# The decay mask of a retention block: made on the chip from two loaded rows instead of loaded as a table

## The chip, the cores and the metric

One core of one Trainium2 chip. The metric is device time in microseconds (us) of one execution; lower is better. Several executions are given by their median. Times inside an execution come from one profiled execution, counted from the start of its span.

## The reference

Three stages follow one another on 2 x 768 tokens: a retention (linear attention with a fixed decay for each of 8 heads of 64 channels), an MLP 512 -> 2048 -> 512 with x·sigmoid(1.702x), and a SwiGLU 512 -> 1536 -> 512 behind an RMS norm.

```python
gamma = 1.0 - 2.0 ** (-5.0 - np.arange(H))
for t in range(S):
    state = gamma * state + outer(k[:, :, t], v[:, :, t])
    y[:, :, t] = scale * (q[:, :, t] @ state)
h = y @ w_in;  x1 = (h * sigmoid(1.702 * h)) @ w_out
xn = x1 / sqrt(mean(x1 ** 2) + 1e-6) * rms_g
out = (silu(xn @ w_gate) * (xn @ w_val)) @ w_out2
```

The MLP's and the SwiGLU's weight matrices arrive as 64-bit floats; the kernel brings them to float32 on the chip.

## The kernel before

The retention is computed in 12 chunks of 128 tokens (6 for each of the two sequences). Within a chunk, the scores of k and q for the 8 heads are one product (L319, 8 calls in float32, which the trace shows as 16 matmuls; even heads lie on partitions 0 to 63 and odd ones on 64 to 127), and VectorE multiplies them by a constant table, the decay mask `dm_sb` of 128 x 2 x 4 x 128 float32 (L333): scale·gamma^(t-s) where the query's token t is not before the key's token s, and 0 elsewhere. The masked scores times v give the output of the chunk (`intra`, L369); for all chunks but a sequence's first there is a second part from the state (`inter`, L356), which reads `qd`, the queries times `qd_sb` (made by GpSimd, L281). The state is brought on by `update_products` (L413), which reads `kd`, the keys times `sm_sb` (GpSimd, L288), by a decay on ScalarE (L421) and a sum on VectorE (L429, L431).

The opening (L850 to L965) is written out by hand: the loads, then chunks 0 to 3 of the retention mixed with the conversion of the first weights (tiles `w`, L189 to L222), and the first product of the MLP (`in_proj`, L467). `in_order(opening)` (L965) keeps the instructions of TensorE, VectorE, ScalarE and GpSimd in the order in which the opening writes them; SP's DMA queue isn't in that list. Everything behind the opening is put in order by a scheduler when the program is built; instructions of later lines may be placed among the opening's where their engine is free and nothing orders them. Two of these are on ScalarE: `mean_w` (L1075) and the scaling of the RMS norm's weights in place, `g_sb` (L1076).

Nearly all loads are issued by SP's queue, in the order of the code: q and k of chunk 0 (`qk`, 512 KB), one half of the mask (256 KB), qk of chunk 1, the other half, v and k of chunk 0 (`kv`, two pieces), v of chunk 1, `qd_sb`, qk of chunk 2, and so on to the tiles of chunk 5. ScalarE's queue issues two small ones: `sm_sb` (12 numbers on each of 128 partitions, 6 KB) and `g_sb` (4 numbers on each, 2 KB). The first work of TensorE are 8 products of a constant (`warming(WARM)`, L859), whose result nobody reads.

Of the kernel before, what the change touches and what calls it, by code (L numbers as in the profile page):

```python
# [8 lines left out]
F32 = mybir.dt.float32  # L9
# [6 lines left out]
ALU = mybir.AluOpType  # L16
# [3 lines left out]
C = 128  # L20
NC = S // C
NP = H // 2
DM = H * D
NT = B * S
KD = DM // 128
F1 = 2048 // 128
F2 = 1536 // 128
T = 512
# [14 lines left out]
WITH_WR = (0, 1, 2, 3, 4, 5, 6, 10, 11, 12)  # L43
JOIN = 4
HELD = 2
WARM, MORE = 8, 0
ENGINES = [mybir.EngineType.PE, mybir.EngineType.DVE, mybir.EngineType.Activation, mybir.EngineType.Pool]
SPLIT = [mybir.EngineType.DVE, mybir.EngineType.Activation]
WAIT = mybir.DependencyInfo(mybir.DependencyClass.Sync, mybir.DependencyReason.DATA)
# [4 lines left out]
def tile_retention_mlp_swiglu(  # L54
# [19 lines left out]
    nc = tc.nc  # L74
# [6 lines left out]
    xt_p = pool("xt", 1)  # L81
# [5 lines left out]
    ps_t = pool("ps_t", 2, space=PSUM)  # L87
# [6 lines left out]
    dm_sb = at_p.tile([128, 2, NP, C], F32, name="dm_sb")  # L94
    qd_sb = at_p.tile([128, NP, C], F32, name="qd_sb")
    S_two = [at_p.tile([128, NP, D], F32, name=f"S_sb{n}") for n in range(2)]
    sm_sb = const.tile([128, 12, 1], F32, name="sm_sb")
    g_sb = const.tile([128, KD], F32, name="g_sb")
# [9 lines left out]
    def psum(p, name):  # L108
        return p.tile([128, T], F32, tag=p.name, name=name)
# [156 lines left out]
    def load_kv(c, parts=None):  # L266
        if ("kv", c) not in ld:
            p, tag = (wr_p, "wr") if c < CPB else (ld_p, "ld")
            ld["kv", c] = p.tile([128, 2, H, D], F32, tag=tag, name=f"kv{c}")
        t = ld["kv", c]  # L270
        if parts is None and c >= 2:
            nc.sync.dma_start(out=t.rearrange("p a h d -> p (a h d)"), in_=kv[c])
            return
        for n in parts or (1, 0):
            nc.sync.dma_start(out=t[:, n].rearrange("p h d -> p (h d)"), in_=kv[c][:, n * T:n * T + T])
# [36 lines left out]
    def score_products(c, p):  # L312
        t = ld["qk", c]
        sc = at["sc", c] = [psum(p, f"sc{c}_{e}") for e in range(2)]
        begun = len(nc.cur_bb.bb.instructions)
        earlier = of(mybir.EngineType.PE)[-1]
        for n in range(NP):
            for e in range(2):
                nc.tensor.matmul(  # L319
                    out=sc[e][:, n * C:(n + 1) * C],  # L320
                    lhsT=t[64 * e:64 * e + 64, 1, n, :],
                    rhs=t[64 * e:64 * e + 64, 0, n, :],
                    start=True,
                    stop=True,
                )
        if c > CPB:
            after(of(mybir.EngineType.PE, begun)[0], earlier)

    def masks(c):
        sc = at.pop(("sc", c))  # L330
        for e in range(2):
            a = tmp(f"a{c}_{e}")
            nc.vector.tensor_tensor(  # L333
                out=a, in0=sc[e], in1=dm_sb[:, e].rearrange("p n c -> p (n c)"), op=ALU.mult
            )
            at["a", c, e] = a
# [373 lines left out]
    fill = deque()  # L710
# [146 lines left out]
    def warming(n):  # L857
        for _ in range(n):
            nc.tensor.matmul(out=warm, lhsT=one(128), rhs=one(T), start=True, stop=True)  # L859

    def load_mask(e):
        o = slice(e * T, e * T + T)
        nc.sync.dma_start(out=dm_sb.rearrange("p e n c -> p (e n c)")[:, o], in_=dmask[:, o])

    warming(WARM)
    load_qk(0)
    load_mask(0)
    load_qk(1)
    load_mask(1)
    load_kv(0)  # L870
    nc.scalar.dma_start(out=sm_sb.rearrange("p n o -> p (n o)"), in_=small)
    load_kv(1, (1,))
    nc.sync.dma_start(out=qd_sb.rearrange("p n c -> p (n c)"), in_=qdec)
    load_qk(2)
# [4 lines left out]
    load_kv(3)  # L879
    for _ in range(3):  # L880
        load_next()
    nc.scalar.dma_start(out=g_sb, in_=rms_g)
    load_qk(CPB)
    load_kv(CPB)
    load_qk(CPB + 1)
    load_kv(CPB + 1)

    nc.scalar.activation(out=first, in_=ones[:, 0:1], func=ACTF.Silu)
    score_products(0, ps_a)
    score_products(1, ps_a)  # L890
    warming(MORE)
    masks(0)
    prep_k(0)
    intra(0, ps_h)
    masks(1)
# [16 lines left out]
    r = convert_next(split=True)  # L912
# [461 lines left out]
```

## Time and profile before

| | us |
|---|---|
| median of three executions (lowest, highest) | 585.52 (585.43, 586.13) |
| the profiled execution, its own time | 585.22 |
| its span | 583.4 |
| TensorE busy in the span | 575.7 |

The span runs from the first to the last instruction of the profiled execution; its own time holds 1.82 us more. A matmul's busy time includes waiting in TensorE's pipeline, so that two of them overlap; what the engine did not do is read from the idle times.

### The profile page before, as it was taken

To read this page: it belongs to the slowest core of one execution; us is meant where nothing else is said; L and a number is where in the kernel's file an instruction comes from. 1 tells how busy PE (TensorE), PEld (TensorE's weight loads), DVE (VectorE), ACT (ScalarE), POOL (GpSimd) and SP (SyncE) were. 2 spreads that over 40 slices of the span, in tenths; PEclk is the share of its full clock that TensorE was granted. 3 is DMA by queue.
4 is the path that set the end of the run, shared out by engine and by line. 5 is a ranking of instruction groups with operands and counts; after the bars stand their busy time and mean duration, and the time that the engine had idled before them with its cause. 6 is when DMAs were issued, how large, how long until landed. Compare 5 with 4: busy or idle time off the path is not lost.

```text
span 583.4 us, 9280 instructions
## 1 busy us (share of the span) xinstructions
PE 575.7 (99%) x3274; PEld 481.1 (82%) x3274; DVE 450.7 (77%) x806; ACT 365.4 (63%) x697; POOL 24.5 (4%) x26
## 2 busy tenths in 40 slices
PE   7999999999999999999999999999999999999997
PEld 5887887888788888878888888988989889988885
DVE  3899998879989888367998998888958676644542
ACT  2878776667687887466647875666645446634442
POOL 3300212100000000000000000000000000000000
PEclk9999999999999999999999999999999999999999
DMA  8999999888369899878744336676414476560412
GB/s 321 408 287 379 391 325 370 276 258 311 115 238 317 285 328 349 306 246 315 290 162 165 108 122 203 200 230 220 163 61 138 145 273 247 201 207 11 152 65 74
DMA packets 48287, 135.11 MB, mean 232 GB/s; under 512 B 5616, under 2 KB 5872, under 8 KB 48240
## 3 DMA queue, kind: packets, MB, share of 16 engines
q1 hardware_dynamic: 47808, 134.37, 66.0%
q8 instruction: 26, 0.43, 0.3%
q14 instruction: 21, 0.17, 0.1%
q10 hardware_dynamic: 432, 0.14, 0.1%
HBM read 98.84 MB, written 35.65 MB: 231 GB/s over the span
## 4 chain that ended last, share of the span: by engine, by line
PE 97%; DMA 2%; ACT 0%; DVE 0%; issue 0%; ACTq 0%
PE acc L444 8%; PE h L467 8%; PE acc L446 7%; PE acc L445 7%; PE o L444 6%; PE o L445 6%; PE o L446 6%; PE sc L319 2%; PE y L356 2%; PE y L369 2%; DMA qk<-in_qk 1%; PE m7a L778 1%; PE v0a L778 1%; PE m0a L778 1%; PE m1a L778 1%; PE g10a L778 1%
## 5 line engine op out<-in xcount | busy, mean ns | idle before, releaser
L445 PE MATMUL o<-w,gh 128*128 128x512 f32 x144 | 56.2, 390 | 0.0
L444 PE MATMUL o<-w,gh 128*128 128x512 f32 x144 | 56.2, 390 | 0.0
L446 PE MATMUL o<-w,gl 128*128 128x512 f32 x144 | 56.1, 389 | 0.0
L201 DVE CUSTOM_DVE_ANT_0 qw<-qw,uw 128x1024 uint16<-128x1024 uint16 x67 | 45.9, 686 | 2.6 <-ACT uw L199 0.5
L198 ACT ACTIVATE qw<-w 128x512 f32<-128x512 f32 x67 | 44.6, 665 | 2.6 <-DMA w<-in_w 2.6
L199 ACT ACTIVATE uw<-w 128x512 uint32<-128x512 uint32 x67 | 44.7, 668 | 0.0
L450 DVE TENSOR_TENSOR gl<-gw,gh 128x512 fp32r<-128x512 f32 x24 | 16.6, 691 | 27.1 <-ACT gh L449 27.0
L200 DVE TENSOR_SCALAR qw<-qw 128x512 uint32<-128x512 uint32 x67 | 28.8, 431 | 9.9 <-ACT qw L198 9.8
L449 ACT ACTIVATE gh<-gw 128x512 fp32r<-128x512 f32 x24 | 15.1, 630 | 28.0 <-PE o L445 22.5
L446 PEld LDWEIGHTS o<-w,gl 128*128 128x128 f32 x144 | 27.0, 188 | 5.7
L445 PEld LDWEIGHTS o<-w,gh 128*128 128x128 f32 x144 | 27.1, 188 | 4.6
L444 PEld LDWEIGHTS o<-w,gh 128*128 128x128 f32 x144 | 27.1, 188 | 4.5
L444 PE MATMUL acc<-gh,wo 128*128 128x512 f32 x64 | 25.9, 412 | 0.0
L446 PE MATMUL acc<-gh,wo 128*128 128x512 f32 x64 | 25.0, 391 | 0.0
L445 PE MATMUL acc<-gl,wo 128*128 128x512 f32 x64 | 25.0, 391 | 0.0
L445 PE MATMUL acc<-gl,wowp 128*128 128x512 f32 x64 | 24.9, 389 | 0.0
L446 PE MATMUL acc<-gh,wowp 128*128 128x512 f32 x64 | 24.9, 389 | 0.0
L444 PE MATMUL acc<-gh,wowq 128*128 128x512 f32 x64 | 24.9, 389 | 0.0
L445 PE MATMUL acc<-gl,wowq 128*128 128x512 f32 x64 | 24.9, 389 | 0.0
L446 PE MATMUL acc<-gh,wowq 128*128 128x512 f32 x64 | 24.9, 389 | 0.0
L207 DVE SCALAR_TENSOR_TENSOR qw<-w,qw 128x512 uint32<-128x512 uint32 x36 | 24.7, 686 | 0.2
L467 PE MATMUL h<-xt0h,wih 128*128 128x512 f32 (+2 forms) x68 | 24.8, 387 | 0.0
(1519 smaller groups left out, 1691.4 us busy)
## 6 DMA issues: line engine op xcount, KB each, us to landing
w<-in_w SPq DMA_DIRECT2D x68, 512.0 KB, 6.2
qk<-in_qk SPq DMA_DIRECT2D x12, 512.0 KB, 7.6
kv<-in_kv SPq DMA_DIRECT2D x10, 512.0 KB, 8.5
gmd<-gm SPq DMA_DIRECT2D x16, 256.0 KB, 4.4
gwm<-gmd SPq DMA_DIRECT2D x16, 256.0 KB, 4.5
g1d<-gs SPq DMA_DIRECT2D x12, 256.0 KB, 2.1
g2d<-gl SPq DMA_DIRECT2D x12, 256.0 KB, 2.6
gw<-g1d SPq DMA_DIRECT2D x12, 256.0 KB, 3.4
```

What stands on the lines that cost most here:

```text
L198: lambda: nc.scalar.activation(out=q, in_=high.bitcast(F32), func=ACTF.Copy, scale=2.0 ** -112),
L199: lambda: nc.scalar.activation(out=t, in_=low, func=ACTF.Copy, scale=2.0 ** -29),
L200: lambda: nc.vector.tensor_scalar(out=m, in0=m, scalar1=3, scalar2=None, op0=ALU.logical_shift_left),
L201: lambda: nc.vector.tensor_tensor(out=m, in0=m, in1=t, op=ALU.add),
L207: nc.vector.scalar_tensor_tensor(out=dst, in0=high, scalar=0x80000000, in1=m, op0=ALU.bitwise_and, op1=ALU.bitwise_or)
L444: nc.tensor.matmul(out=out, lhsT=ah, rhs=bh, start=first, stop=False)
L445: nc.tensor.matmul(out=out, lhsT=ah, rhs=bl, start=False, stop=False)
L446: nc.tensor.matmul(out=out, lhsT=al, rhs=bh, start=False, stop=last)
L449: nc.scalar.activation(out=hi, in_=src, func=ACTF.Copy)
L450: nc.vector.tensor_tensor(out=lo, in0=src, in1=hi.bitcast(F32), op=ALU.subtract)
L467: nc.tensor.matmul(out=ps[:, begin:end], lhsT=w[a][:, k * 128:(k + 1) * 128], rhs=x[b][:, k, begin:end], start=begin == 0 and o == order[0 ...
L778: nc.tensor.matmul(out=bank, lhsT=u, rhs=v, start=first and k == 0 and x == 0, stop=k == 1 and x == 2, skip_group_check=True,)
```

## The change

Both halves of the mask's load go away. Instead:

- ScalarE's queue loads two things into a tile called `rows`, on partitions 0 and 64 alone: the whole of `small` (1536 numbers, its first eight columns being gamma_h^(127-s) by token s and head h) and one row of `qdec` (512 numbers, scale·gamma_h^(t+1) by head pair and token t) for the even and for the odd heads.
- VectorE fills the mask's tile with gamma_h^(-128) (8 memsets), and GpSimd sets it to 0 where the query's token lies before the key's (2 affine_selects).
- TensorE makes 8 outer products of one partition each (float32, 128 x 128), whose stationary operand is read from `rows` in steps of 12 numbers, into two PSUM tiles; VectorE multiplies each by the constant triangle, in place (2 operations of 128 x 512).
- These products stand ahead of chunk 0's scores on TensorE, and the two multiplications ahead of chunk 0's masking on VectorE.
- `sm_sb` is loaded third on ScalarE's queue, behind that engine's first activation, where it was the first.
- `g_sb` is loaded by SP's queue behind the tiles of chunk 5, where ScalarE's queue loaded it second.
- 6 warming products stand where there were 8; `masks(0)` is written ahead of chunk 1's scores (each engine's own order stays as it was by that).

```diff
-WARM, MORE = 8, 0
+WARM, MORE = 6, 0
...
-    def load_mask(e):
-        o = slice(e * T, e * T + T)
-        nc.sync.dma_start(out=dm_sb.rearrange("p e n c -> p (e n c)")[:, o], in_=dmask[:, o])
+    rows = xt_p.tile([128, KD, T], F32, tag="xt1h", name="rows")
+    by_token = rows[:, 0:3, :].rearrange("p k t -> p (k t)").rearrange("p (t n) -> p t n", n=12)
+    ends_of = slice(0, 65, 64)
+    nc.scalar.dma_start(
+        out=rows[ends_of, 0:3, :].rearrange("p k t -> p (k t)"),
+        in_=small.rearrange("t n -> (t n)").unsqueeze(0).to_broadcast([2, 12 * C]),
+    )
+    nc.scalar.dma_start(out=rows[ends_of, 3, :], in_=qdec[ends_of, :])
+    for e in range(2):
+        for n in range(NP):
+            nc.vector.memset(dm_sb[:, e, n, :], (1.0 - 2.0 ** (-5.0 - (2 * n + e))) ** -C)
+        nc.gpsimd.affine_select(
+            out=dm_sb[:, e], in_=dm_sb[:, e], pattern=[[0, NP], [1, C]], compare_op=ALU.is_ge,
+            fill=0.0, base=0, channel_multiplier=-1,
+        )
+
+    def mask_products():
+        lags = [psum(ps_t, f"lag{e}") for e in range(2)]
+        for n in range(NP):
+            for e in range(2):
+                r = slice(64 * e, 64 * e + 1)
+                nc.tensor.matmul(
+                    out=lags[e][:, n * C:(n + 1) * C],
+                    lhsT=by_token[r, :, 2 * n + e],
+                    rhs=rows[r, 3, n * C:(n + 1) * C],
+                    start=True,
+                    stop=True,
+                )
+        for e in range(2):
+            t = dm_sb[:, e].rearrange("p n c -> p (n c)")
+            nc.vector.tensor_tensor(out=t, in0=lags[e], in1=t, op=ALU.mult)
...
     load_qk(0)
-    load_mask(0)
     load_qk(1)
-    load_mask(1)
     load_kv(0)
-    nc.scalar.dma_start(out=sm_sb.rearrange("p n o -> p (n o)"), in_=small)
...
-    nc.scalar.dma_start(out=g_sb, in_=rms_g)
     load_qk(CPB)
     load_kv(CPB)
     load_qk(CPB + 1)
     load_kv(CPB + 1)
+    nc.sync.dma_start(out=g_sb, in_=rms_g)
 
     nc.scalar.activation(out=first, in_=ones[:, 0:1], func=ACTF.Silu)
+    nc.scalar.dma_start(out=sm_sb.rearrange("p n o -> p (n o)"), in_=small)
+    mask_products()
     score_products(0, ps_a)
+    masks(0)
     score_products(1, ps_a)
-    warming(MORE)
-    masks(0)
     prep_k(0)
```

## Rows read from the trace of the kernel before

**Rows 1.** The page: span, and the engines' busy time.

```profile
span 583.4 us, 9280 instructions
...
PE 575.7 (99%) x3274; PEld 481.1 (82%) x3274; DVE 450.7 (77%) x806; ACT 365.4 (63%) x697; POOL 24.5 (4%) x26
```

**Rows 2.** Busy time by stretch: each engine's, granted clock, DMA share, GB/s.

```profile
8.70:12.00 3.30, 2.66 (x48) 2.34 (x49) 1.51 (x4) 0.60 (x1) 2.31 (x2) 1.00 1.06 407
...
0.00:12.01 12.01, 8.94 (x89) 5.71 (x89) 2.94 (x6) 2.49 (x5) 2.79 (x9) 1.00 0.85 302
12.01:36.00 23.99, 23.47 (x278) 20.04 (x279) 20.52 (x37) 20.55 (x50) 7.23 (x6) 1.00 1.00 372
...
320.00:583.40 263.40, 259.35 (x1378) 223.86 (x1376) 185.56 (x352) 143.10 (x283) 0.00 (x0) 1.00 0.47 156
```

**Rows 3.** The chain that ended last, 0 to 40 us: start, length, what.

```profile
1.18 4.92 DMA g_sb<-in_rms_g
...
6.11 5.76 DMA qk<-in_qk
```

**Rows 4.** Timeline of PE: start, length, instruction, idle time before it and its releaser.

```profile
0.77 3.57 PE L859 MATMUL warm<-const-bfloat16-1.0 128*128 128x512 bf16 x8 [0.77 <-PEq L1367]
4.41 1.55 PE L319 MATMUL sc<-qk 64*128 64x128 f32 x16
7.25 1.16 PE L319 MATMUL sc<-qk 64*128 64x128 f32 x16 [1.30 <-DMA qk<-in_qk]
...
10.05 1.09 PE L369 MATMUL y<-a,kv 128*64 128x128 f32 x16 [0.24 <-DMA kv<-in_kv]
10.95 0.66 PE L413 MATMUL u<-kv,kd 128*64 128x64 f32 x16
12.01 1.16 PE L319 MATMUL sc<-qk 64*128 64x128 f32 x16 [0.40 <-DMA qk<-in_qk]
```

**Rows 5.** Timeline of DVE, its first work.

```profile
6.01 0.69 DVE L333 TENSOR_TENSOR a<-sc,dm_sb 128x512 f32<-128x512 f32 x1 [6.01 <-PE sc L319]
7.97 1.89 DVE L333 TENSOR_TENSOR a<-sc,dm_sb 128x512 f32<-128x512 f32 x3 [1.27 <-DMA dm_sb<-in_dmask]
```

**Rows 6.** Timeline of POOL, its first work behind the constants.

```profile
9.37 1.04 POOL L288 TENSOR_TENSOR kd<-kv,sm_sb 128x512 f32<-128x512 f32 x1 [8.36 <-DMA kv<-in_kv]
10.65 1.27 POOL L281 TENSOR_TENSOR qd<-qk,qd_sb 128x512 f32<-128x512 f32 x1 [0.24 <-DMA qd_sb<-in_qdec]
```

**Rows 7.** Timeline of ACT, 0 to 10 us.

```profile
2.95 0.20 ACT L888 ACTIVATE first<-ones 128x1 f32<-128x1 f32 x1
...
6.12 0.21 ACT L1076 ACTIVATE g_sb<-g_sb 128x4 f32<-128x4 f32 x1 [2.77 <-DMA g_sb<-in_rms_g]
```

**Rows 8.** DMA issues, 0 to 25 us: count, KB each, median us to landing.

```profile
dm_sb<-in_dmask SPq DMA_DIRECT2D x2, 256.0 KB, 5.3
...
sm_sb<-in_small ACTq DMA_DIRECT2D x1, 6.0 KB, 3.8
g_sb<-in_rms_g ACTq DMA_DIRECT2D x1, 2.0 KB, 4.9
```

**Rows 9.** Timeline of SP's queue, three of its issues.

```profile
0.74 0.39 SPq L263 DMA_DIRECT2D qk<-in_qk  x1
...
2.59 2.33 SPq L275 DMA_DIRECT2D kv<-in_kv  x3
...
16.39 0.33 SPq L272 DMA_DIRECT2D kv<-in_kv  x1
```

**Rows 10.** Waits of SP's queue, 0 to 40 us: total, times, longest.

```profile
SPq L275 <- DMA sm_sb<-in_small: 1.0, 1, 1.0
...
SPq L263 <- DMA g_sb<-in_rms_g: 0.6, 1, 0.6
```

**Rows 11.** Line 319, 4 to 6.5 us: ns of one, min/median/max.

```profile
L319 PE MATMUL sc<-qk x16: 272/283/576, 4.4 to 5.7; 64*128 64x128 f32 x16
```

**Rows 12.** Tile kv, 0 to 40 us: its loads' time to landing.

```profile
DMA to landing us min/median/max: 5.3/6.6/11.5
```

## The prediction

> **What bounds the kernel now.** I read the page first, then the busy time by stretch, the chain of waits, and the engines' timelines of the opening. TensorE is busy for 575.7 of 583.4 us [rows 1]; of the 7.7 us that it stands still, 3.07 lie before 12.01 us, 0.52 between there and 36 us, and 4.05 behind 320 us, mostly the last evacuation and store [rows 2]. So behind 12 us the kernel runs at TensorE's pace, and whatever moves the start of chunk 2's scores at 12.01 us [rows 4] moves the end by as much, as long as the loads and the other engines come earlier too. The change touches only what lies ahead of that point.
>
> What sets 12.01 us? The chain of waits passes through two transfers: g_sb's, 1.18 to 6.10 us, and qk of chunk 2, 6.11 to 11.87 [rows 3]. The first link is a queue's: the ninth and later loads wait for the landing of the one eight issues before. Counted in order of issue over both queues, v of chunk 1 is the ninth and stands behind sm_sb, qk of chunk 2 the eleventh and stands behind g_sb, fourth [rows 9, 10]. That link cost SP 0.6 us. The second link is bandwidth: from 8.70 us on the 16 engines are full at 407 GB/s [rows 2], so a load lands when the bytes ahead of it are through.
>
> A second chain lies just under it. VectorE's first masking starts at 6.01 us, the next waits 1.27 us for the mask's second half, and the four end at 7.97 + 1.89 = 9.86 us [rows 5]. `intra` of chunk 1 starts at 10.05 (for v of chunk 1), the state's update at 10.95 and takes 0.66, so TensorE would have been free at 11.61 had qk not been late by 0.40 [rows 4]. Anything saved on loads alone above 0.40 us therefore needs this second chain to move too.
>
> **The change part by part.**
>
> *The mask's load goes.* 2 x 256 KB [rows 8] = 524 kB at 407 GB/s [rows 2] = 1.29 us that everything behind both halves lands earlier: qk of chunk 2 at 10.58 for 11.87 [rows 3], v of chunk 1 at 8.8 for 10.05 [rows 4], k of chunk 0 at 8.1 for 9.37, qd_sb at 9.3 for 10.65 [rows 6]. qk of chunk 1 has one half ahead of it, so 0.64: 6.6 for 7.25 [rows 4]. With the 0.14 us from landing to the first product (11.87 to 12.01), chunk 2's scores can't start before 10.72: the loads cap the gain at 1.29 us.
>
> *g_sb leaves the front.* This frees one of the eight places early. Since the engines are full anyway I count 0; it is worth at most the 0.6 us that SP stood behind it [rows 10], so the cap may reach 1.89.
>
> *The rows' loads.* They are issued where sm_sb and g_sb were, the second at 1.18 us. Landing: g_sb took 4.9 from there [rows 8], which gives 6.1 at the latest; the first qk was issued at 0.74 and its scores start at 4.41, 3.67 us in which 524 kB moved (1.29 at 407 GB/s), so some 2.4 for a tiny load, 3.6 us at the earliest [rows 2, 4, 9]. They are four long pieces and not 256 short ones, so nearer the lower end, but share the engines with qk: I take 4.2.
>
> *The outer products.* Eight float32 calls of the scores' shape but for the rows. These take 1.16 us at TensorE's upper level, and chunk 0's took 1.55, its slowest matmul 576 ns against 272 [rows 4, 11]: it began at the lower level. The warming products show that level: 3.57/8 = 0.446 us for 512 columns [rows 4], 1.2 GHz, whatever the granted clock says there (1.00) [rows 2]. Six of them end at 0.77 + 6 x 0.446 = 3.45 us, so TensorE stands still for some 0.8 us ahead of the products, where before it ran on into the scores and the level rose during them. All at the lower level would be 2.3. I take the mixed 1.55; the ends are 1.16 and 2.3. So the products end at L = 4.2 + 1.55 = 5.75 us.
>
> The scores' operands, which that row of 1.16 us is of, are read in unit steps [rows 4]. [...]
>
> *VectorE's chain.* It now does six operations before chunk 1 can go on: two by the triangle, four maskings. Spacing (1.89 - 0.69)/2 = 0.60, the last 0.69 [rows 5]: 0.05 + 5 x 0.60 + 0.69 = 3.74 us after L, if scores are ready in time; chunk 0's end at L + 1.16 and the third operation starts at L + 1.25, and chunk 1's at L + 2.3 and the fifth at L + 2.45. So the maskings end at 9.49, for 9.86 before.
>
> *To chunk 2.* `intra` of chunk 1 at 9.54 (its v landed at 8.8), the update 0.90 later at 10.44, and 0.66 behind it chunk 2's scores at 11.10 [rows 4]; their qk is there at 10.58. In one line, start = L + 5.35 but not before 10.72. 12.01 - 11.10 = **0.91 us gained**. It equals the old time where L = 6.66.
>
> *Hidden edits.* The 8 memsets and 2 affine_selects: VectorE has nothing before 6.01 [rows 5] and GpSimd nothing between the constants and 9.37 [rows 6]. GpSimd's own operations of this size took 1.04 and 1.27 us [rows 6]; two from about 1.5 us end at 4.1. The first must be there at L = 5.8, the second 0.6 later, so each may take up to 2.4 before it costs anything. Two warming products fewer: they lie where TensorE waits; their price is the clock above. `sm_sb` third: ScalarE reaches it at 2.95 + 0.20 [rows 7]; with a landing of 3.8 to 4.9 [rows 8] it is there at 7.4 to 8.5 with the issue, as k of chunk 0 is (8.1). `kd` then takes 1.04 and is needed at 10.44: about 0.9 us of slack. `g_sb` behind chunk 5: its reader, the norm, comes after 200 us, but its scaling on ScalarE is the fourth rival.
>
> Sum against the profiled execution: 585.22 - 0.91 = 584.3; that execution lies 0.30 under the median of 585.52. Against the median: 584.6. I allow 0.1 for a clock that rises a little later, since TensorE does less before the products: **584.7 us**. What this kernel can tell from no change is about 0.2%, 1.17 us: under 584.35 is faster, over 586.69 slower.
>
> **The rivals.**
>
> 1. *The loads set it* (0.22). The rows land near 3.6 us or the products take 1.16, so L is at most 5.37, and the second chain is under the first: start 10.72, gain 1.29, with g_sb's place up to 1.89. 583.6 to 584.2. For it: the chain of waits names the loads today. Against: the second chain has to give way by all of 0.9 us.
> 2. *The products are slow* (0.21), by the steps of 48 bytes or by a clock that stays low through chunk 0's scores. [...] With the scores at 2.3 as well, the maskings wait for these: L = 6.5, scores 8.8, and the four maskings 0.05 + 3 x 0.60 + 0.69 later 11.3, chunk 2 at 12.9, 0.9 lost, 586.4. [...] For it: the pause ahead of the products and the steps; against: the engine has ended its warming less than 1 us before.
> 3. *sm_sb comes late* (0.08). Issued among SP's loads it is counted among the eight: if it takes a place behind v of chunk 0, say, ScalarE's queue stands until that has landed, about 7 us, and sm_sb is there at 11 to 12. `kd` ends 1.04 later, and the update that had to start at 10.44 starts at 12 to 13: chunk 2 at 12.7 to 13.7, 0.7 to 1.7 lost, 586.2 to 587.2. It costs from a landing at 9.4 on.
> 4. *ScalarE stands behind g_sb* (0.09), my case on the other side. The scaling L1076 isn't ordered behind the opening; before, it was placed among the opening's activations and ScalarE stood 2.77 us for the load, harmlessly, ahead of an engine without work [rows 7]. Now the load is issued behind chunk 5's, whose last is issued at 16.39 us [rows 9] and lands up to 11.5 us later [rows 12]: some 26 us after the 1.29. If the scaling is again placed at its old point or in a gap of chunk 1 or 2, ScalarE stands until then, and with it chunk 0's or 1's outputs and the first weights: 8 to 16 us lost, 593 to 601. It decides as soon as ScalarE comes to L1076 before some 26 us. Against it I have no row, only that such a place needs the scheduler to be wrong about the landing by 10 us and more.
>
> **How the numbers follow.** My forecast, gains of 0.3 to 1.2 us, has 0.40 (584.3 to 585.2), of which a fifth is under 584.35. Faster: 0.22 + 0.08 = 0.30. Slower: the fourth rival's 0.09, half of the third's 0.08, and a third of the second's 0.21: 0.20. The same: 0.50. The range goes from the first rival's lower middle, 583.8, to the end of the third, 587.2; the fourth stays out. The likeliest case alone is 584.3 to 585.2.
>
> **What the profile after would show.** Right: chunk 2's scores start near 11.1 us, with VectorE's maskings of chunk 1 ending near 9.5 and qk of chunk 2 landing at 10.6; the outer products begin at 4.2 and last 1.5; later stages alike, shifted. Wrong: weight loads of the outer products far longer than those of the scores, matmuls of 576 ns in chunk 0's scores to the end, GpSimd's `kd` waiting for sm_sb, ScalarE waiting for g_sb, or new idle time on TensorE between 12 and 36 us. The forecast also fails if the order behind the opening comes out differently and adds waits there, which this trace cannot show.

## The result and the profile after

The changed kernel takes 589.13 us (median of 6 runs, 588.48 to 590.01), beside 585.47 for the kernel before in the same comparison: ratio 1.006, interval 1.0047 to 1.0073. It is slower by 3.7 us; 584.7 was forecast, with a range to 587.2. On the chips of the experiments the kernel before fell into two groups, 585.3 to 587.5 us (87 of 120 runs) and 589.4 to 593.3, so that the ratios there have wide intervals; its lower group alone has a median of 585.9 (e1 to e4), 586.2 (e5 to e12) and 586.0 (e13, e14), and sizes are read from the profiles.

The page of the changed kernel, whose profiled execution took 588.48 us (585.22 before):

```profile
span 586.6 us, 9325 instructions
...
PE 578.2 (99%) x3288; PEld 484.1 (83%) x3288; DVE 453.1 (77%) x816; ACT 365.0 (62%) x697; POOL 25.7 (4%) x28
```

Its busy time by stretch, cut at the start of chunk 2's scores, now 15.85 us; columns as in [rows 2]:

```profile
4.40:5.60 1.20, 0.00 (x0) 0.00 (x0) 0.00 (x0) 0.00 (x0) 0.00 (x0) 1.00 0.70 224
0.00:15.85 15.85, 11.67 (x103) 8.95 (x103) 5.02 (x14) 2.28 (x4) 7.55 (x15) 1.00 0.88 333
15.85:39.10 23.25, 23.25 (x280) 19.82 (x279) 20.11 (x36) 19.73 (x50) 3.25 (x3) 1.00 0.90 310
323.10:586.60 263.50, 259.38 (x1378) 223.90 (x1377) 185.64 (x352) 143.31 (x283) 0.00 (x0) 1.00 0.46 156
```

The span grew by 3.2 us [rows 1]: TensorE is busy 2.5 us longer and stands still 0.7 longer (8.4 for 7.7). The standing has moved: 4.18 us ahead of chunk 2's scores for 3.07, none in the 23 us behind them for 0.52, 4.12 at the end for 4.05 [rows 2]. So the whole loss was made ahead of 15.85 us. Its timeline of TensorE says where [rows 4]:

```profile
0.84 2.72 PE L859 MATMUL warm<-const-bfloat16-1.0 128*128 128x512 bf16 x6 [0.84 <-PEq L1393]
6.76 2.52 PE L882 MATMUL lag<-rows 1*128 1x128 f32 x16 [3.20 <-DMA rows<-in_qdec]
9.21 3.78 PE L319 MATMUL sc<-qk 64*128 64x128 f32 x32
12.92 2.43 PE L369 MATMUL y<-a,kv 128*64 128x128 f32 x31
...
15.85 1.16 PE L319 MATMUL sc<-qk 64*128 64x128 f32 x16
```

Three things are new: 3.20 us of waiting for the rows, products of 2.52 us, and both scores in 3.78 us without a pause in them, where before they were 1.55 and 1.16 (2.71) around a wait for qk. Chunk 2's scores start 3.84 us later than before; the two later stages that I compared start 3.1 us later (the MLP's second product, L444, at 35.02 for 31.91; `m0a`, L778, at 141.43 for 138.29). In the compared stretch behind chunk 2's start TensorE no longer waits (0.52 us before) and is busy 23.25 us for 23.47: together 0.74. In the kernel before:

```profile
138.29 0.62 PE L778 MATMUL m0a<-xm,wm0xh 128*128 128x512 f32 x2
```

The second row load in the chain that ended last [rows 3], and ScalarE's queue [rows 7]:

```profile
1.94 4.68 DMA rows<-in_qdec
```

```profile
0.80 1.11 ACTq L864 DMA_DIRECT2D rows<-in_small  x1
1.94 0.50 ACTq L868 DMA_DIRECT2D rows<-in_qdec  x1
...
2.55 0.40 ACTq L914 DMA_DIRECT2D sm_sb<-in_small  x1
```

The issue of the first row load took 1.11 us, so the second was issued at 1.94, not at 1.18 as I had it; it landed 4.68 later, at 6.62. The engines were not full meanwhile: 0.70 between 4.4 and 5.6 us, at 224 GB/s (the first row of the windows above).

The products and the scores by the duration of one (min/median/max in ns): first the products, then the scores of chunks 0 and 1, then those of chunk 2 [rows 11].

```profile
L882 PEld LDWEIGHTS lag<-rows x16: 337/364/368, 6.7 to 8.6; 1*128 1x128 f32 x16
...
L319 PEld LDWEIGHTS sc<-qk x32: 285/330/330, 9.2 to 12.4; 64*128 64x128 f32 x32
L319 PE MATMUL sc<-qk x32: 414/418/579, 9.2 to 12.6; 64*128 64x128 f32 x32
...
L319 PE MATMUL sc<-qk x16: 272/272/373, 15.8 to 16.7; 64*128 64x128 f32 x16
```

One and the same instruction takes 418 ns up to 12.6 us and 272 from 15.8 on. The granted clock reads 1.00 in all these stretches, as it did before [rows 2], so here the level is read from durations: TensorE ran its six warming products of 512 columns in 2.72 us (0.43 us from start to start; in e1 below the last 8 of 17 took 2.02), stood still for 3.20 us, and was at the lower level, 418 ns, through all scores. In e6, e14 and e3 below the granted clock itself reads 0.50, beside long durations again: both scores take 3.78 us in e6, and 2.89 in e3 for 2.06 in e1; in e14 31 matmuls of `intra` take 4.06 for 2.43. In the kernel before, TensorE went from the warming into the scores without such a pause (0.07 us), and chunk 1's 16 took 1.16 us [rows 4].

VectorE [rows 5] and GpSimd [rows 6] in the opening:

```profile
11.31 1.29 DVE L333 TENSOR_TENSOR a<-sc,dm_sb 128x512 f32<-128x512 f32 x2 [0.68 <-PE sc L319]
13.02 1.29 DVE L333 TENSOR_TENSOR a<-sc,dm_sb 128x512 f32<-128x512 f32 x2 [0.42 <-PE sc L319]
```

```profile
1.56 1.22 POOL L872 TENSOR_SCALAR_AFFINE_SELECT dm_sb<-dm_sb 128x512 f32<-128x512 f32 x2 [0.49 <-DVE dm_sb L871]
8.04 1.04 POOL L288 TENSOR_TENSOR kd<-kv,sm_sb 128x512 f32<-128x512 f32 x1 [5.26 <-DMA sm_sb<-in_small]
```

The masks now wait for scores twice (0.68 and 0.42 us): TensorE is behind VectorE. The triangle is done early, and `kd` waits for sm_sb to 8.04, before it is needed.

### The profile page after: what moved, and what is told of

The parts are those of the page before. It is cut to its first block, busy times and chain, and to the rows that moved or that the text cites. A ratio compares the mean times of both kernels' runs of the same rounds, so it can differ in the third digit from the quotient of the medians.

```text
span 586.6 us, 9325 instructions
## 1 busy us (share of the span) xinstructions
PE 578.2 (99%) x3288; PEld 484.1 (83%) x3288; DVE 453.1 (77%) x816; ACT 365.0 (62%) x697; POOL 25.7 (4%) x28
## 4 chain that ended last, share of the span: by engine, by line
PE 98%; DMA 1%; DVE 0%; ACT 0%; ACTq 0%; issue 0%
PE acc L444 8%; PE h L467 8%; PE acc L446 7%; PE acc L445 7%; PE o L445 6%; PE o L446 6%; PE o L444 6%; PE sc L319 3%; PE y L369 2%; PE y L356 2%; PE m7a L778 1%; PE v0a L778 1%; PE m0a L778 1%; PE g10a L778 1%; PE g8a L778 1%; PE g6a L778 1%
## 5 line engine op out<-in xcount | busy, mean ns | idle before, releaser
L444 PE MATMUL o<-w,gh 128*128 128x512 f32 x144 | 56.2, 390 | 0.0
L444 PEld LDWEIGHTS o<-w,gh 128*128 128x128 f32 x144 | 27.1, 188 | 4.7
L444 PE MATMUL acc<-gh,wo 128*128 128x512 f32 x64 | 25.9, 412 | 0.0
L207 DVE SCALAR_TENSOR_TENSOR qw<-w,qw 128x512 uint32<-128x512 uint32 x36 | 24.7, 687 | 0.2
L444 PE MATMUL acc<-gh,wowq 128*128 128x512 f32 x64 | 24.9, 389 | 0.0
```

The lines of the kernel that those rows point to most:

```text
L207: nc.vector.scalar_tensor_tensor(out=dst, in0=high, scalar=0x80000000, in1=m, op0=ALU.bitwise_and, op1=ALU.bitwise_or)
L444: nc.tensor.matmul(out=out, lhsT=ah, rhs=bh, start=first, stop=False)
```

## The experiments

The theories at the start: A, TensorE's pause and the lower level behind it set the loss; B, the stationary operand's 48-byte steps and the late rows set it; C, rms_g's new place costs by itself; D, what is saved ahead of chunk 2 does not reach the end. Each time beside a ratio is a median.

**e1_warm17: warming products until the rows land.**

```diff
-WARM, MORE = 6, 0
+WARM, MORE = 17, 0
```

> The changed kernel with 17 warming products for 6, so that TensorE doesn't stand still before the rows land (6.62 us). In the changed kernel chunk 2's scores start at 15.85 us, 3.84 later than before. Theory A (the clock: the pause of 3.2 us ahead of the outer products keeps TensorE at its lower level until about 13 us): the products take about 1.2 us for 2.52, chunks 0 and 1's scores about 2.3 for 3.78, chunk 2's scores start near 13.3, and the kernel takes about 2.5 us less than the changed one, 586.6. Theory B (the steps of 48 bytes in the stationary operand make the products slow): they stay above 2.2 us, chunk 2's scores start no earlier than 14.5, 588 us. Theory C (only the late landing of the rows counts): nothing moves by more than 0.5 us.

588.19 us beside 586.03, ratio 1.0018 (0.9984 to 1.0052). TensorE now goes from the warming into the products:

```profile
6.60 2.42 PE L882 MATMUL lag<-rows 1*128 1x128 f32 x16
8.95 2.06 PE L319 MATMUL sc<-qk 64*128 64x128 f32 x32
...
14.32 1.16 PE L319 MATMUL sc<-qk 64*128 64x128 f32 x16
```

The scores fall from 3.78 to 2.06 us and chunk 2 starts 1.53 us earlier, 0.16 of it ahead of the products (6.60 for 6.76): the pause and the level behind it cost this much there. The products keep 2.42 of their 2.52: their time is not the level's. So A was right on the scores and wrong on the products, B the other way round. Less is seen at the end: the span is 586.1 us, 0.5 under the changed kernel's.

**e2_warm17_unit: the same, with the stationary operand read in unit steps** (other numbers, so the mask's values are not the reference's).

```diff
-                    lhsT=by_token[r, :, 2 * n + e],
+                    lhsT=rows[r, (n + 2 * e) % 3, 0:C],
```

> As the run with 17 warming products, and the outer products read their stationary operand from the rows in unit steps; they multiply other numbers so, and the mask is not the reference's. Theory A (clock alone): products and total as in that run within 0.3 us. Theory B (steps of 48 bytes): the products take 1.2 us, at least 1 us less than in that run, and the total falls by as much.

587.37 us beside 586.03, ratio 1.0009 (0.9988 to 1.0031). The products' loads and the timeline:

```profile
L882 PEld LDWEIGHTS lag<-rows x16: 181/187/187, 6.8 to 7.6; 1*128 1x128 f32 x16
```

```profile
6.80 1.16 PE L882 MATMUL lag<-rows 1*128 1x128 f32 x16 [0.39 <-DMA rows<-in_qdec]
...
13.26 1.16 PE L319 MATMUL sc<-qk 64*128 64x128 f32 x16
```

A load of weights takes 187 ns for 364, the products 1.16 us for 2.42: 1.26 us are the steps of 48 bytes, of which 1.06 reach chunk 2; the span is 585.4. By these rows a load in such steps takes 1.95 times as long as one in unit steps.

**e3_rows_on_sp: the two row loads first on SyncE's queue, ahead of chunk 0's q and k, with 8 warming products.**

```diff
-    nc.scalar.dma_start(
+    nc.sync.dma_start(
         out=rows[ends_of, 0:3, :].rearrange("p k t -> p (k t)"),
...
-    nc.scalar.dma_start(out=rows[ends_of, 3, :], in_=qdec[ends_of, :])
+    nc.sync.dma_start(out=rows[ends_of, 3, :], in_=qdec[ends_of, :])
```

> The changed kernel with the two loads of the rows issued by SP's queue ahead of chunk 0's q and k, and 8 warming products. Their issues took 1.11 and 0.50 us on ScalarE's queue, so the first qk is issued 1.6 us later. Theory C (the landing of the rows is what went wrong, and their place behind a full queue is why): they land by 4.5 us, the products run from there at the clock of the kernel before, scores from about 6.2, chunk 2's scores near 12.3: 585.8 us, within 0.5 of before. If the rows are late for another reason (the form of the transfer), they land after 5.5 again and the total stays over 587.

590.65 us beside 586.03, ratio 1.0062 (1.0033 to 1.0091). The products start at 4.34, right behind the warming, and still take 2.41 us; chunk 2's scores start at 12.63, only 0.62 later than before. The row loads, then TensorE:

```profile
0.81 0.65 SPq L864 DMA_DIRECT2D rows<-in_small  x1
1.51 0.49 SPq L868 DMA_DIRECT2D rows<-in_qdec  x1
```

```profile
4.34 2.41 PE L882 MATMUL lag<-rows 1*128 1x128 f32 x16
```

The second load was issued at 1.51 us and used without a wait at 4.34, at most 2.8 us later, where in the changed kernel it took 4.68. The pieces are the same; what differs is the queue, and that no load of q and k is issued ahead of it. So the rows can be there at 4.2, as was forecast, but not from their place in the change.

The time is the worst of all nonetheless. At L444 the kernel is 0.45 us behind the one before; then TensorE waits 3.26 us at 95 us, and behind the wait runs at the lower level again (granted clock 0.50 from 100 to 102 us). Its waits list:

```profile
PE y L356 <- DVE a L333: 3.3, 1, 3.3
```

So a better opening can be lost behind it: theory D has a case, though rms_g is moved here as in e4, which has a wait at the same place.

**e4_g_alone: the kernel before with rms_g alone moved**, to SyncE's queue behind chunk 5's tiles, as the change does.

```diff
-    nc.scalar.dma_start(out=g_sb, in_=rms_g)
...
     load_kv(CPB + 1)
+    nc.sync.dma_start(out=g_sb, in_=rms_g)
```

> The kernel before with one part of the change alone: rms_g loaded by SP's queue behind chunk 5's tiles. My prediction's term: 0, at most 0.6 us earlier landing of chunk 2's q and k, of which 0.40 can reach TensorE: 585.1 to 585.5. Rival: SP's later loads or ScalarE's scaling suffer from it: 586 or more.

588.22 us beside 586.03, ratio 1.0018 (0.9989 to 1.0046). TensorE's waits, and ScalarE's first conversion of a weight, in the kernel before and here:

```profile
PE y L356 <- DVE a L333: 1.7, 1, 1.7
...
PE y L369 <- DMA kv<-in_kv: 1.2, 2, 0.9
```

```profile
16.40 0.67 ACT L189 ACTIVATE qw<-w 128x512 f32<-128x512 f32 x1
```

```profile
18.10 0.67 ACT L189 ACTIVATE qw<-w 128x512 f32<-128x512 f32 x1 [1.50 <-DMA w<-in_w]
```

The kernel with the edit that I costed at nothing is some 2.3 us slower (all ten runs at 587.5 us or more; the span is 3.0 us longer). SP issues the loads in the same order as before, so no other load has come ahead of the first weight's. Of that load's 16 parts, as the trace's semaphore counts them, 15 had landed by 16.48 us, and the last at 18.08; the conversion waited for that one. In the kernel before all 16 were there by 16.38, and the next load, chunk 3's k and v, had its last part late, by 1.15 us. Both traces have, in this stretch, one packet of the queue that the profile calls "instruction", of 16 KB and 1.1 us:

```profile
q8 instruction: 1, 0.02, 1.7%
```

That this packet makes the late part, and that rms_g's place decides which load it hits, fits the two traces but was not tested. Chunk 3 waits 0.9 us for its tile, and the conversion of weights starts 1.7 us late. The 1.7 us at 95 us stand behind a conversion of VectorE (L207) that took 1.78 us for its usual 0.69 while GpSimd worked beside it (L281, 1.74 us from 92.83 on); that the late conversion leads there was not isolated. The opening differs as well: behind the same 8 warming products chunk 0's scores took 2.08 us here and 1.55 in the kernel before.

**e5_g_back: the changed kernel with rms_g on ScalarE's queue behind small.**

```diff
     nc.scalar.dma_start(out=sm_sb.rearrange("p n o -> p (n o)"), in_=small)
+    nc.scalar.dma_start(out=g_sb, in_=rms_g)
...
-    nc.sync.dma_start(out=g_sb, in_=rms_g)
```

> The changed kernel with one part undone: rms_g loaded by ScalarE's queue again, behind sm_sb. Moving that load alone, on the kernel before, cost about 2.2 us of time (588.2 for 586.0), though chunk 2's scores started only 0.15 us later: the first weight tile landed 1.7 us later and TensorE stood 1.71 us at 95.6 us. Theory D (in the changed kernel this cost is hidden behind the 3.84 us by which chunk 2 starts late): undoing it changes the total by less than 0.6 us. Theory E (the two costs add): the total falls by about 2 us, to 586.9.

588.84 us beside 586.35, ratio 1.0044 (1.0027 to 1.0061). Chunk 2's scores at 15.40 (15.85), products 2.52, scores 3.45. So in the changed kernel rms_g's place neither makes nor mends the loss; e4's loss isn't found on top of it.

**e6_from_qdec: the outer products from qd_sb's own rows, in unit steps**, with VectorE's reciprocal as the other factor, qd_sb loaded first, no row loads, 8 warming products, small and rms_g as before.

```diff
+    nc.sync.dma_start(out=qd_sb.rearrange("p n c -> p (n c)"), in_=qdec)
     load_qk(0)
...
+        nc.vector.reciprocal(out=back, in_=qd_sb[0:65].rearrange("p n c -> p (n c)"))
...
+                    out=lags[e][:, n * C:(n + 1) * C], lhsT=back[r, n * C:(n + 1) * C], rhs=qd_sb[r, n, :],
```

> A version meant to do what the change intended: no rows are loaded; qd_sb is loaded first, VectorE takes its reciprocal (one operation on 65 partitions), and the outer products multiply reciprocal and qd_sb, both in unit steps, under a triangle of 1/8. sm_sb, g_sb and the 8 warming products stay as before. By the prediction's own chain, qd_sb lands near 3.7 us, the products run from 4.4 to 5.9, chunk 2's scores start at 11.2, 0.8 us earlier than before; the total 0.5 to 0.8 us less if the end follows, and equal if the weights' conversion can't.

588.71 us beside 586.35, ratio 1.0036 (1.0018 to 1.0053). The load landed at 3.5 as expected, the reciprocal did not keep to its estimate:

```profile
3.53 3.35 DVE L875 RECIPROCAL back<-qd_sb 65x512 f32<-65x512 f32 x1 [1.49 <-DMA qd_sb<-in_qdec]
```

```profile
6.93 2.00 PE L880 MATMUL lag<-qd_sb,back 1*128 1x128 f32 x16 [2.84 <-DVE back L875]
8.86 3.78 PE L319 MATMUL sc<-qk 64*128 64x128 f32 x32
```

TensorE again stood 2.84 us, again ran at the lower level (granted clock 0.50 from 8.0 to 11.8 us), and the scores took the same 3.78. Unit steps give 2.00 us here, so in the changed kernel the steps cost 0.5 of the 2.52; at the upper level they cost 1.26 (2.42 for 1.16). The load in steps took about the same in both: 364 ns in the changed kernel, 365 in e1.

**e7_warm17_unit_gback: e2 with rms_g as in e5.**

```diff
-WARM, MORE = 6, 0
+WARM, MORE = 17, 0
...
-                    lhsT=by_token[r, :, 2 * n + e],
+                    lhsT=rows[r, (n + 2 * e) % 3, 0:C],
...
+    nc.scalar.dma_start(out=g_sb, in_=rms_g)
```

> The changed kernel with 17 warming products, with the stationary operand read in unit steps (so its mask is not the reference's) and with rms_g loaded by ScalarE's queue again. The run with the first two alone started chunk 2 at 13.26 us, 1.25 later than before, but ended 2.0 us later. Theory D: without the moved load that surplus goes, so chunk 2 at 13.3 and the end about 1.3 us over before at most: 586.5 beside 586.0. If the surplus stays (end 2 us over), it isn't g_sb's place that makes it.

586.86 us beside 586.35, ratio 0.9988 (0.9961 to 1.0016): with steps, level and rms_g all mended the times can't tell it from the kernel before, but the span, 584.9, is still 1.5 longer. Chunk 2's scores start at 13.1, still 1.1 late: the wait for the rows and the products at full speed, 1.16 us.

**e8_no_mask_load: the kernel before without the mask's load**, the constant triangle in its place (the mask's values are not the reference's).

```diff
     load_qk(0)
-    load_mask(0)
     load_qk(1)
-    load_mask(1)
```

> The kernel before without the mask's two loads; a constant triangle stands in the mask's place, so the scores are not decayed as in the reference. It shows what the removed bytes are worth by themselves. My prediction's cap: everything behind them lands up to 1.29 us earlier, chunk 2's scores start at 10.7 to 11.1 and the kernel gains as much, 0.9 to 1.3 us. Rival: TensorE comes earlier but the conversion of the weights (VectorE, ScalarE, their loads) can't follow, and less than 0.5 us arrives at the end.

584.79 us beside 586.35, ratio 0.996 (0.9933 to 0.9987):

```profile
10.55 1.16 PE L319 MATMUL sc<-qk 64*128 64x128 f32 x16
```

Chunk 2's scores start 1.46 us earlier, `m0a` 1.44 earlier (136.85), and the span is 1.3 shorter (582.1). The removed bytes are worth a little more than the prediction's cap for them, 1.29 with rms_g where it was (the 1.89 is for rms_g moved): 1.46, and here nearly all of it reaches the end.

**e9_mask_by_exp: the whole mask made by GpSimd and ScalarE**, with no load and no product: the lag t - s in a 128 x 128 tile, eight Exps of it.

```diff
-    load_mask(0)
...
-    load_mask(1)
...
+    nc.gpsimd.iota(lag, pattern=[[1, C]], base=0, channel_multiplier=-1, allow_small_or_imprecise_dtypes=True)
+    nc.gpsimd.affine_select(
+        out=lag, in_=lag, pattern=[[1, C]], compare_op=ALU.is_ge, fill=1e6, base=0, channel_multiplier=-1,
+    )
...
+            nc.scalar.activation(
+                out=dm_sb[:, e, n, :], in_=lag, func=ACTF.Exp, bias=eighth,
+                scale=float(math.log1p(-2.0 ** (-5.0 - (2 * n + e)))),
+            )
```

> The kernel before, with the mask neither loaded nor made by TensorE: GpSimd writes the lag t - s into a 128x128 tile, sets it to a million where it is negative, and ScalarE makes the eight masks as Exp(lag x ln gamma + ln(1/8)), all before the first scores are masked. Nothing else moves (rms_g, small and the warming products as before). Theory (the removed bytes are worth 1.44 to 1.53 us, and what the changed kernel lost went to TensorE's wait, its slow products and its lower level): ScalarE loads a table by 3.0 us, makes eight masks of about 0.29 us each by 5.3 us (row of mean_w, 128x128: 0.29 us) and loads the second table by 6.6 us, before its next work at 9.0; chunk 2's scores start at 10.5 to 10.7 (12.01 before), the span is 582.1 +-0.4 and the ratio to before 0.996 to 0.998. Rival (anything that makes the mask on the chip delays the first masks, VectorE's work at 6.5 us): the Exps end behind 6.5 us, chunk 2's scores start at 12 or later, and the ratio is 1.000 or more.

588.93 us beside 586.60, ratio 1.0017 (0.9987 to 1.0047): a miss, for two reasons. The Exps stood behind the scaling of rms_g, as my fourth rival feared for ScalarE:

```profile
5.96 0.20 ACT L1089 ACTIVATE g_sb<-g_sb 128x4 f32<-128x4 f32 x1 [2.70 <-DMA g_sb<-in_rms_g]
6.07 2.43 ACT L896 ACTIVATE dm_sb<-lag,eighth 128x128 f32<-128x128 f32 x8
```

Chunk 2's scores start at 11.96. And TensorE, which had no wait behind that, did less in the same time: `m0a` starts at 138.04 (138.29 before), and the span is 3.0 us longer. One stretch of e9's busy time, in which e13 below does 432 matmuls:

```profile
138.00:236.00 98.00, 98.00 (x427) 79.45 (x427) 87.50 (x162) 76.13 (x140) 0.00 (x0) 1.00 0.79 270
```

**e10_after_again: the changed kernel on that chip.** No edit.

> The changed kernel itself, beside the others on this chip, so that they stand against one run of before. By its first comparison the ratio is 1.006; the theories do not differ: TensorE's outer products start at 6.7 +-0.3 and last 2.5, both scores 3.4 to 3.8, chunk 2's scores start at 15.4 to 15.9, span 586.6 +-0.8.

588.97 us beside 586.60, ratio 1.001 (0.998 to 1.0039). Products at 6.81, 2.52 us; scores 3.79; chunk 2 at 15.89; span 587.2: the first profile again up to chunk 2, and 0.6 us longer at the end, lost between L444 and `m0a`. So differences of that size at the end are not to be read from one profile.

**e11_warm6_alone: the kernel before with two warming products fewer.**

```diff
-WARM, MORE = 8, 0
+WARM, MORE = 6, 0
```

> The kernel before with 6 warming products for 8, nothing else: the price of the edit that the prediction costed at nothing. Theory A (TensorE's level after the warming decides how fast the first scores run): the pause ahead of the first scores grows from 0.07 us to about 0.8, TensorE does not rise to its upper level in them, and the scores of chunks 0 and 1 take 2.0 instead of 1.55 and 1.16 to 2.0 each; chunk 2's scores start 0 to 1.2 us later, the span is 583.4 to 584.8. Rival (the first scores wait for their loads anyway): chunk 2's scores start at 12.01 +-0.15, the ratio is 1.000 +-0.001.

586.78 us beside 586.60, ratio 0.9979 (0.9945 to 1.0014): the times can't tell. The profile can:

```profile
4.28 2.08 PE L319 MATMUL sc<-qk 64*128 64x128 f32 x16 [0.79 <-DMA qk<-in_qk]
7.39 2.08 PE L319 MATMUL sc<-qk 64*128 64x128 f32 x16 [1.04 <-DMA qk<-in_qk]
...
12.67 1.16 PE L319 MATMUL sc<-qk 64*128 64x128 f32 x16
```

Six warming products and a pause of 0.79 us behind them leave TensorE at the lower level through both scores (2.08 each, for 1.55 and 1.16), and chunk 2 starts 0.66 later; the span is 584.1, 0.7 longer. The fewer products and the pause were not separated. Chunk 1's row carries the reading: with 8 warming products chunk 0's scores took 1.16 to 2.08 us over the traces (1.16 in e13, 2.08 in e4), chunk 1's 1.16 in each.

**e12_after_no_products: the changed kernel without row loads and products** (constant triangle only), 8 warming products.

```diff
-    nc.scalar.dma_start(
-        out=rows[ends_of, 0:3, :].rearrange("p k t -> p (k t)"),
...
-    nc.scalar.dma_start(out=rows[ends_of, 3, :], in_=qdec[ends_of, :])
...
-    mask_products()
```

> The changed kernel without the two loaded rows and without the outer products (the mask is the constant triangle alone, so its values are not the reference's), with 8 warming products: what is left of the change is the mask that isn't loaded, small behind the other loads, and rms_g behind chunk 5's tiles on SyncE's queue. If the whole loss of the changed kernel came from rows, products and clock, this gives the removed bytes' gain: chunk 2's scores at 10.5 to 10.8, span 582.1 +-0.5, ratio 0.996 to 0.998. If rms_g's new place costs by itself what it cost in the kernel before (one 512 KB load ahead of the first weight tile, a stall of TensorE of 1.7 us near 95 us, 2.2 to 3.3 us in all), chunk 2's scores start as early, but the span is 584.3 to 585.4 and the ratio 1.000 to 1.003, with the loss behind 40 us.

585.93 us beside 586.60, ratio 0.9942 (0.9914 to 0.997), 12 runs within 0.7 us; beside 586.2 that is a gain of only 0.3 us. Chunk 2's scores start at 10.76, L444 at 30.50 (1.41 earlier than before), but `m0a` at 138.29, the same time as before: the gain is paid back between, at least 0.8 us of it at the next use of a converted weight. TensorE's waits behind 20 us:

```profile
PE h L467 <- ACT wih L449: 0.5, 1, 0.5
PE h L467 <- DVE wil L450: 0.3, 1, 0.3
```

The span is 584.1, 0.7 us over the kernel before's and 2.0 over that of e8, which differs from it in the place of rms_g and small.

**e13_mask_by_exp_first: e9 mended**: the Exps ahead of rms_g's scaling, the constant in a column of a tile that exists anyway.

```diff
-    eighth = const.tile([128, 1], F32, name="eighth")
+    eighth, lag = lag[:, 1, 0:1], lag[:, 0, 0:C]
...
     nc.scalar.activation(out=g_sb, in_=g_sb, func=ACTF.Copy, scale=FACTOR)
+    after(nc.cur_bb.bb.instructions[-1], made)
```

> The mask by Exp once more, mended in two places that its first version got wrong: the Exps stand ahead of the scaling of rms_g in ScalarE's stream (there they stood behind it, until 6.07 us), and the constant ln(1/8) lies in a column of a tile that exists anyway, so that no tile's address moves (there a new 4-byte tile moved the tiles behind it, and TensorE's matmuls stood 229 to 232 ns apart instead of 226.7 between 150 and 480 us). Theory (late Exps cost the first 1.5 us, shifted addresses the last 3): the Exps run from 3.3 to 5.7 us, chunk 2's scores start at 10.4 to 10.8 (12.01 before), every later stage is 1.2 to 1.6 us earlier than before, the span is 582.0 +-0.5. Rival (the slower matmuls came from something else in this form, and a table load more on ScalarE): chunk 2's scores start as early, but the span is 585 or more.

585.33 us beside 586.19, ratio 0.997 (0.9949 to 0.9991), 12 runs within 1.4 us: beside 586.0 a gain of 0.6 us by the times, and faster than the changed kernel. TensorE, then ScalarE:

```profile
6.25 1.16 PE L320 MATMUL sc<-qk 64*128 64x128 f32 x16 [0.95 <-DMA qk<-in_qk]
...
10.56 1.16 PE L320 MATMUL sc<-qk 64*128 64x128 f32 x16 [0.22 <-DMA qk<-in_qk]
...
17.89 1.09 PE L370 MATMUL y<-a,kv 128*64 128x128 f32 x16 [0.93 <-DVE qw L192]
```

```profile
3.17 2.43 ACT L896 ACTIVATE dm_sb<-lag 128x128 f32<-128x128 f32 x8
...
16.66 0.66 ACT L190 ACTIVATE qw<-w 128x512 f32<-128x512 f32 x1 [1.66 <-DMA w<-in_w]
```

The first masking starts at 5.41 us. 1.45 us are gained up to chunk 2, 0.70 still there at L444 (31.21) and 0.30 at `m0a` (137.99): VectorE's first conversion now makes TensorE wait 0.93 us, since ScalarE's waits 1.66 us for the weight. As in e4, 15 of the load's 16 parts were there early, by 14.68 us, and the last at 16.63, with a packet of the queue "instruction", of 1.1 us, in between. The span is 583.4, the kernel before's: the gain that the times show is not in the profiled execution. My span of 582.0 was too low by 1.4. The slower matmuls of e9 are gone (432 in that stretch); which of the two edits removed them was not separated, the moved tiles being the likelier, since ScalarE's order ends at 10 us.

**e14_products_last: the changed kernel with the products behind both scores**, 8 warming products.

```diff
-    mask_products()
     score_products(0, ps_a)
-    masks(0)
     score_products(1, ps_a)
+    mask_products()
+    masks(0)
```

> The changed kernel with its outer products behind the scores of chunks 0 and 1 instead of ahead of them, and with 8 warming products; loads as in the changed kernel. TensorE then does not stand before the first scores. Theory A (the pause and the lower level behind it set the loss): the scores run from 4.35 us in 2.6 to 3.1 us, the products follow at 7.0 to 7.5 in 1.2 to 2.5, chunk 2's scores start at 13.0 or earlier and the span is 584.0 to 585.0. Theory B (the loaded rows' landing near 6.6 us and the products' 48-byte steps set it, since the masks need them whatever TensorE does meanwhile): the products end at 9.4 to 9.9, the mask table at 10.8 to 11.2, chunk 2's scores start at 14.6 to 15.3, and the span is 585.4 to 586.2.

589.46 us beside 586.19, ratio 1.0042 (1.0019 to 1.0065). Neither theory had it:

```profile
7.40 2.41 PE L882 MATMUL lag<-rows 1*128 1x128 f32 x16
11.86 4.06 PE L369 MATMUL y<-a,kv 128*64 128x128 f32 x31 [2.05 <-DVE a L333]
...
16.92 1.59 PE L319 MATMUL sc<-qk 64*128 64x128 f32 x16
```

```profile
11.86:15.51 3.65, 3.65 (x32) 3.34 (x34) 1.74 (x3) 0.60 (x1) 3.27 (x3) 0.50 1.03 413
```

The scores ran early and at the upper level (1.16 each), the products kept 2.41. The masks waited for the products, TensorE stood 2.05 us for the masks, and came back at the lower level: 4.06 us for 2.43, granted clock 0.50. The pause has moved, not gone. So here the late path (B) makes the pause, and the lower level (A) follows it; they are one loss in two parts. In the changed kernel the warming products started 0.43 us apart up to the pause; in e1, with the pause filled, the last 8 took 2.02 us and the scores 2.06.

## Why the prediction was wrong

The forecast was that chunk 2's scores start at 11.10 us, from rows landing at 4.2, products of 1.55, and 5.35 us from their end. Measured: 6.76, 2.52, and 15.85 - 9.28 = 6.57. The three misses are 2.56 + 0.97 + 1.22 = 4.75 us, which is 15.85 - 11.10.

- *The rows' landing at 4.2: failed, the largest term.* My upper bound, 6.1, counted g_sb's 4.9 us from an issue at 1.18; the trace has the issue at 1.94, behind 1.11 us for the first load's, and 4.68 to the landing. e3 shows what made it late: first in the queue the same pieces were used at 4.34 without a wait, so it was their place, on ScalarE's queue beside and behind the loads of q and k, and not their form. Being four long pieces brought them nothing in that place. I took a value near the lower bound for a transfer that the nearest row put at the upper one.
- *The outer products at 1.55 us: failed.* The 48-byte steps, of which the rows of the kernel before have no load and which the 1.55 leaves out, are shown by e1 and e2: 2.42 against 1.16 with TensorE at the upper level. Behind its pause, e6 shows 2.00 with unit steps; the changed kernel has 2.52.
- *"Two warming products fewer: their price is the clock above": undersized.* I let the pause grow to 0.8 us and the level rise during the products. The pause was 3.20 us, because the rows were late, and the level rose only behind both scores: 3.78 us for 2.06 in e1, and chunk 2 1.53 us later. The forecast's 1.2 GHz is 512 columns in the 0.43 us from one warming product's start to the next; no row gives TensorE's clock in GHz. Of the third miss, 1.22 us from the products' end to chunk 2, 1.10 are VectorE's two waits for these scores (0.68 and 0.42), which the forecast put at nothing ("if scores are ready in time"). e11 lost 0.66 us of chunk 2's start to its six products and the 0.79 us behind them.
- *The second rival named mechanism and place, and was too small:* it started its sum from rows at 4.2, and came to 0.9 us lost by products and scores that stay slow. It had 0.21; with the rows' upper bound, 6.1, in it, it would have said over 2 us.
- *The cap of the loads: near.* It was 1.29 us with rms_g where it was; e8 has 1.46 at chunk 2 and 1.3 at the span's end.
- *Hidden edits:* memsets and affine_selects right (the triangle is done at 1.56 + 1.22 = 2.8 us); sm_sb right (7.9 us, within 7.4 to 8.5, and harmless). *g_sb's place at 0: wrong for the kernel of e4* (some 2.3 us), by a cause that was not isolated; e12 has 2.0 us of span over e8, but small's place differs there too, and in the changed kernel it can't be seen (e5). A slip: g_sb was counted fourth among ScalarE's loads, but by the prediction's own count, the eleventh load waiting for the third, it must stand third, as the trace has it. No term hangs on it.
- *ScalarE behind g_sb: did not happen*; its scaling ran at 28.61 us without a wait.
- *"Whatever moves chunk 2's scores moves the end by as much": right for e8, roughly for the change (3.84 became 3.1), wrong in general.* Of e1's 1.53 us 0.5 are left at the span's end. An earlier start meets the conversion of weights, which did not move with it (e12, e13).

Together, with chunk 2's scores at 15.85: 1.53 us go with the pause and TensorE's level behind it (e1), 1.06 more with the steps (e2), and the remaining 2.71 down to e8's 10.55 are the rows' wait and the products themselves at full speed. The last part was not split further. These are sizes at chunk 2; less of each arrives at the end.

## What to carry to other kernels

Before a load is traded for work on the chip, cost the path from the issue to the first use of what the new work needs, with the nearest small load's landing as the value and not as the far bound: here 16 KB on two partitions landed at 6.6 us, while of the loaded mask the first half had been there for VectorE's work at 6.0. Issued ahead of the big loads, as in e3, they were used at 4.3. Waits of TensorE were paid twice here, once as the wait and again in what ran at the lower level behind it: 3.20 us and then scores of 3.78 for 2.06 in the changed kernel, 2.05 us and then 4.06 for 2.43 in e14, 2.84 us and then scores of 3.78 in e6, and in e3 3.26 us with a granted clock of 0.50 from 100 to 102 us. The table that waits for nothing (an iota and eight Exps on engines without work) is the version that gained, by 0.6 of 586 us.

## What the runs showed of the hardware

- A weight load of 128 float32 numbers in steps of 48 bytes took 364 ns in after, where the scores next to it took 418 each, and 365 in e1 and e14, where the scores next to it took 2.06 us for 32 and 1.16 for 16. In unit steps it took 187 in e2; the scores' loads took 330 in after and e11, and 188 in the kernel before (medians).
- Behind six warming products and a pause of 0.79 us 16 scores took 2.08 us (e11), behind six and a pause of 3.20 both scores 3.78 (after). The granted clock read 0.50 behind a pause of 2.05 us (e14, 11.86 to 15.51), of 2.84 (e6, 8.0 to 11.8) and of 3.26 (e3, 100 to 102). Behind one of 0.95 (e13) and 1.30 (before) 16 scores took 1.16 us, and around one of 1.71 (e4) the clock read 1.00 from 60 to 139 us. In e3 it read 0.50 from 8 to 10 us too, with no pause of TensorE since the warming.
- In the opening of after the granted clock read 1.00 while one matmul of the scores took 418 ns, and 272 later.
- VectorE's reciprocal of 65 x 512 float32 took 3.35 us, some five times the 0.69 of a multiplication of 128 x 512.
- The issue of a load onto two partitions of 6 KB each took 1.11 us on ScalarE's queue and 0.65 on SP's (e3); that of 6 KB over 128 partitions took 0.40 on ScalarE's.
- One of the 16 parts of a 512 KB load landed 1.15 us (before), 1.6 (e4) and 1.95 (e13) behind the others, in stretches with a packet of the queue "instruction", of 1.1 us. That the packet is the cause was not tested.
- In e9 TensorE got through 427 matmuls in the 98 us from 138 on and 656 in the 123 us from 332 on, with no wait; in e13 through 432 and 662.
